# Taking the scale of v for two batches from VectorE's maximum instead of ScalarE's sums, in an attention and mixer kernel on one core

## Chip, core and metric

The kernel runs on one core of one Trainium2 chip. The metric is device time in microseconds (us) of one execution. Before the change three runs took 608.84, 609.73 and 610.28 us: the median is 609.73.

## What is computed

```python
def _attn_ref(q, k, v):                 # (8, 8, 576, 64) each
    scores = scale * np.matmul(q, k.transpose(0, 1, 3, 2))
    scores = np.where(mask, scores + bias[None], -1000000000.0)   # causal, 128 wide
    scores = scores - np.max(scores, axis=-1, keepdims=True)
    attn = np.exp(scores)
    attn = attn / (np.sum(attn, axis=-1, keepdims=True) + 1e-09)
    return np.matmul(attn, v)
def _moe_ref(x, w_theta, w_tok_r, w_tok_i, w_ch):   # x: (8, 576, 512), the heads side by side
    theta = x @ w_theta
    zr, zi = x * np.cos(theta), x * np.sin(theta)
    y = np.einsum('ts,bsd->btd', w_tok_r, zr) + np.einsum('ts,bsd->btd', w_tok_i, zi)
    u = x + y
    return u + np.maximum(u @ w_ch, 0.0)
```

## The kernel before, in words

There are eight batches of eight heads. Heads go in pairs, 32 pairs in all. For a pair, TensorE (PE) multiplies q and k into the PSUM tile s_ps (L621), in two groups of query tiles. VectorE (DVE) adds the band and takes each row's extreme (L631: an operation and a read of its accumulator), and ScalarE (ACT) takes the exponential (L635). The first 7 pairs are "early" ones: PE turns the weights (L677), ACT copies them to the tiles pt (L679), and PE multiplies them with v in fp32 (L687). The later pairs split weights and values into two fp16 halves (L644 on ACT and L646 on DVE; L601 on ACT and L603 on DVE), turn the weights by a DMA (L649) and multiply at L705. DVE divides by the row's sum and writes the heads to x_sb (L660, L663, L664).

For each batch the mixer then runs: angles by PE (L757), a reduction of them and sine and cosine (L771 to L785 on ACT and DVE; L779 and L781 are the two sine activations, which need another table of ACT than the exponential), the split of the result into z_hi (ACT, L790) and z_lo (DVE or POOL, L411), the mixing over tokens (PE, L862; what it gives is taken up at L868 to L875) and the channel product (L890), and the sums that go out (L898 to L907).

The weights come in raw, in fp32. Function `unpack` loads one chunk (L422) into one of the raw tiles u, u_spare, xtfa and xtfb, and rebuilds it with two steps on ACT (L426, and L436 where the chunk's number is under LOW_T, LOW_W or LOW_C; otherwise DVE does that second step, L440) and three on DVE (L432, L443, L452). There are 4 chunks of w_theta, 9 of w_tok and 4 of w_ch.

The values v come in groups of four heads, two groups to a batch (L499, tiles vba, vbb, vbc). Function `measure` finds a power of two per head that scales them. It has two ways:

- For the first SUMMED = 2 batches ACT sums the absolute values of each group (L516, with an accumulator that takes a second instruction to read), and DVE and PE turn the two sums into scales: L525, a transpose on PE (L531), L533, L536, a product on PE (L540), L543 and L385.
- For the other six batches DVE takes each head's largest absolute value by a reduction over 1280 elements (L521, one for each group), and a chain of four small DVE operations and one PE product follows (L548, L552, L555, L558, L561).

The order of all this is not written by hand. `Plan` records each step with its engine, an assumed duration and what it depends on; `simulate` makes an order by priorities; `order` then moves the priorities by a table of seeds, NUDGES; and `run` issues each engine's instructions in that order, so that an engine that waits holds up whatever stands behind the waiting instruction. All loads and DMA transposes are issued from SP's queue, and they land in their order there in the stretch that matters. Where the plan has PE idle, `run` puts in "spins" (L367): small products of the tile `white` that nothing uses, whose number follows the idle time of the plan.

Of the kernel before, what the change touches and what calls it, by code (L numbers as in the profile page):

```python
# [36 lines left out]
TURNED = 0  # L37
TRUE = 3
MIXED = 1
SUMMED = 2  # L40
LIFT = 2.0 ** 16
ABS_T = 4
ABS_W = 9
ABS_C = 4
LOW_T = 4
LOW_W = 5
LOW_C = 1
VALUES = ((0, 0), (1, 2))

MAGIC = 1.5 * 2.0 ** 23  # L50
# [2 lines left out]
while RAD * 0.5 > math.pi:  # L53
# [22 lines left out]
ROUNDS = 6  # L76
SELF = {"DVE": 0.115, "ACT": 0.13, "POOL": 0.1}
NUDGES = (
# [6 lines left out]
)  # L85


# [206 lines left out]
def attn_moe_kernel(ctx: ExitStack, tc: tile.TileContext, qt, kt, vx, wth, wtok, wch, band, out):  # L294
    nc = tc.nc
# [12 lines left out]
    plan = Plan()  # L308
# [84 lines left out]
    for h in range(H):  # L393
        plan("DVE", (0.14, 0.13), lambda h=h: nc.vector.tensor_scalar(
            out=bands[:, h], in0=base, scalar1=2.0 ** (2 - h), scalar2=None, op0=ALU.mult), r=[(band_buf, "base")],
            w=[(band_buf, h)], port=True)
# [16 lines left out]
    def unpack(src, c, w, held, last, first, summed, magnitude, lowest, raw_buf=None):  # L413
# [5 lines left out]
        R, E, M = ((raw_buf, k) for k in "rem")  # L419
        ex, low = t[:, 2 * S:2 * S + w], t[:, 3 * S:3 * S + w]  # L420
        powers = ex.bitcast(BF16).rearrange("p (n t) -> p n t", t=2)[:, :, 1]
        issued.append(plan("SP", (0.42, w * 2.55e-3, 2.15), lambda: nc.sync.dma_start(  # L422
            out=t[:, :2 * w], in_=src[:, c, :].bitcast(I32)), w=[R]))
        plan.follow(issued[-1], begin)
        if magnitude:
# [77 lines left out]
    def measure(b):  # L503
# [6 lines left out]
        for k in range(2):  # L510
            vb = group_v[2 * b + k]
            part = most.tile[:, GROUP * k:GROUP * k + GROUP]
            if b < SUMMED:
                spare = hl_ring.tiles[k].bitcast(BF16).rearrange("p a b c -> p (a b c)")[:, :GROUP * NT * 64].rearrange(
                    "p (h c d) -> p h c d", h=GROUP, d=64)
                taken = plan("ACT", (1.26, 0.15), lambda vb=vb, spare=spare, k=k: nc.scalar.activation(  # L516
                    spare, vb.tile[:, :, 1:, :64], AF.Abs, accum_out=spread.tile[:, k:k + 1]), r=[(vb, 0)],
                    w=[(spread, "ab"[k]), (spare_bufs[k], 0)])
                hl_ring.last[k].users.append(taken)
            else:  # L520
                plan("DVE", (1.395, 0.13), lambda vb=vb, part=part: nc.vector.tensor_reduce(  # L521
                    out=part, in_=vb.tile[:, :, 1:, :64], axis=mybir.AxisListType.XY, op=ALU.max,
                    apply_absolute_value=True), r=[(vb, 0)], w=[(most, k)])
        if b < SUMMED:
            plan("DVE", (0.075, 0.13), lambda: nc.vector.tensor_tensor(  # L525
                out=most.tile.rearrange("p (k h) -> p k h", h=GROUP),
                in0=spread.tile[:, :2, None].broadcast_to([128, 2, GROUP]),
# [19 lines left out]
        else:  # L547
# [22 lines left out]
            w=[(rise, 0)], port=True)  # L570
# [342 lines left out]
    def ready(p):  # L913
        if p >= PAIRS:
            return
        load_pair(p)
        if p % PAIRS_OF == 0:
            load_values(p // 2)
            load_values(p // 2 + 1)
            measure(p // PAIRS_OF)  # L920
        pair_weights[p] = {}, {}
        scores(p, pair_weights[p])

    issued = []
# [6 lines left out]
    for c in range(4):  # L931
        unpack(wth, c, DM, held_theta, first=c == 0, last=c == 3, summed=sums, magnitude=c < ABS_T,
               lowest=c < LOW_T)
    halve(held_theta, sums, DM, range(4), tscale, tturn, TURN, "t", wth_hi, wth_lo, theta_w)
    sums = t_ring.take()
    for k, c in enumerate(ORDER):
        unpack(wtok, c, S, held, first=k == 0, last=k == 8, summed=sums, magnitude=k < ABS_W,
               lowest=k < LOW_W, raw_buf=late_ring.take() if k % 4 == 3 else None)
    for g, c in VALUES:
# [5 lines left out]
        w=[(ws_buf, "share")], port=True)  # L945
# [7 lines left out]
    for c in range(4):  # L953
        unpack(wch, c, DM, held_chan, first=c == 0, last=c == 3, summed=sums, magnitude=c < ABS_C,
               lowest=c < LOW_C, raw_buf=late_ring.take())
    halve(held_chan, sums, DM, range(4), cscale, cscale, 1.0, "c", wch_hi, wch_lo, chan_w)
# [84 lines left out]
```

## Time and profile before

| what | value |
|---|---|
| runs before, median | 609.73 us |
| profiled execution, its own time | 614.84 us |
| its span, first to last instruction | 613.0 us |
| PE, DVE, ACT, POOL busy | 97%, 87%, 81%, 25% of the span |
| mean granted PE clock | 0.994 of full |

The profiled execution took 5.1 us more than the median of the runs, 1.8 us of its time lie outside the span. PE's busy share includes the spins. The stretches behave differently: the first 120 us, where the weights are unpacked and the first batches' attention is done, are limited otherwise than the rest.

### The profile page before, as it was taken

To read this page: it belongs to the slowest core of one execution; us is meant where nothing else is said; L and a number is where in the kernel's file an instruction comes from. 1 tells how busy PE (TensorE), PEld (TensorE's weight loads), DVE (VectorE), ACT (ScalarE), POOL (GpSimd) and SP (SyncE) were. 2 spreads that over 40 slices of the span, in tenths; PEclk is the share of its full clock that TensorE was granted. 3 is DMA by queue.
4 is the path that set the end of the run, shared out by engine and by line. 5 is a ranking of instruction groups with operands and counts; after the bars stand their busy time and mean duration, and the time that the engine had idled before them with its cause. 6 is when DMAs were issued, how large, how long until landed. Compare 5 with 4: busy or idle time off the path is not lost.

```text
span 613.0 us, 14313 instructions
## 1 busy us (share of the span) xinstructions
PE 596.3 (97%) x5417; PEld 438.9 (72%) x5417; DVE 531.4 (87%) x1568; ACT 498.8 (81%) x923; POOL 150.4 (25%) x133
## 2 busy tenths in 40 slices
PE   8997999999998999999999999999999999999997
PEld 6786756886676766776677767777677668776775
DVE  5798999999998999899898999999989999658433
ACT  4998999968998889996999689978899699246312
POOL 1000120011240215621474114231232133415100
PEclk9899999999998999999999999999999999999999
DMA  8784762399559892897569775989156734211102
GB/s 313 295 287 148 186 152 57 90 214 183 109 149 218 143 164 68 201 202 165 86 156 226 153 129 120 239 125 209 58 137 143 132 51 108 74 36 39 49 1 78
DMA packets 165541, 87.24 MB, mean 142 GB/s; under 512 B 144736, under 2 KB 153056, under 8 KB 165472
## 3 DMA queue, kind: packets, MB, share of 16 engines
q1 hardware_dynamic: 165472, 86.33, 61.1%
q8 instruction: 42, 0.69, 0.5%
q14 instruction: 27, 0.22, 0.1%
HBM read 41.22 MB, written 9.44 MB: 83 GB/s over the span
## 4 chain that ended last, share of the span: by engine, by line
PE 66%; ACT 18%; DMA 6%; DVE 6%; issue 2%; SPq 1%; POOL 0%; ACTq 0%; DVEq 0%
PE m_psb L862 15%; PE m_psa L862 15%; PE s_ps L621 7%; PE m_psa L890 7%; PE m_psb L890 6%; PE t_psa L757 5%; PE t_psb L757 5%; PE a_psb L705 3%; PE a_psa L705 3%; DMA ptd<-hlb 2%; DMA vbb<-in_vx_dram 2%; ACT sbb L635 2%; ACT sba L635 1%; ACT sbc L635 1%; ACT z_hi L790 1%
## 5 line engine op out<-in xcount | busy, mean ns | idle before, releaser
L862 PEld LDWEIGHTS <-z_hi 128*128 128x128 f16 x1152 | 110.2, 98 | 35.9 <-issue 6.3
L890 PEld LDWEIGHTS <-wch 128*128 128x128 f16 x768 | 73.8, 98 | 24.2 <-issue 4.4
L862 PE MATMUL m_psb<-wtk_hi,z_hi 128*128 128x288 f16 x288 | 82.9, 288 | 0.0
L862 PE MATMUL m_psb<-wtk_hi,z_lo 128*128 128x288 f16 x288 | 82.9, 288 | 0.0
L862 PE MATMUL m_psb<-wtk_lo,z_hi 128*128 128x288 f16 x288 | 82.9, 288 | 0.0
L862 PE MATMUL m_psa<-wtk_hi,z_hi 128*128 128x288 f16 x288 | 82.7, 287 | 0.0
L862 PE MATMUL m_psa<-wtk_lo,z_hi 128*128 128x288 f16 x288 | 82.5, 286 | 0.0
L862 PE MATMUL m_psa<-wtk_hi,z_lo 128*128 128x288 f16 x288 | 82.4, 286 | 0.0
L862 PEld LDWEIGHTS <-z_lo 128*128 128x128 f16 x576 | 56.5, 98 | 14.8 <-DVE z_lo L411 0.3
L411 POOL TENSOR_TENSOR z_lo<-wch_held,z_hi 128x512 f16<-128x512 f32 x28 | 36.8, 1329 | 67.8 <-ACT z_hi L790 67.7
L890 PE MATMUL m_psa<-u,wch 128*128 128x288 f16 x384 | 52.3, 286 | 0.8 <-ACT u_spare L898 0.8
L890 PE MATMUL m_psb<-u,wch 128*128 128x288 f16 x384 | 52.3, 286 | 0.0
L635 ACT ACTIVATE sba<-sba,fixed 128x256 f32<-128x256 f32 (+2 forms) x110 | 44.8, 460 | 3.0 <-DVE fixed L631 2.7
L812 POOL TENSOR_TENSOR hlxa<-x_sba,hlxa 128x512 f16<-128x512 f32 (+1 forms) x12 | 15.4, 1279 | 126.4 <-ACT hlxa L811 126.3
L635 ACT ACTIVATE sbc<-sbc,fixed 128x256 f32<-128x256 f32 (+2 forms) x106 | 43.3, 459 | 3.0 <-DVE fixed L631 2.9
L635 ACT ACTIVATE sbb<-sbb,fixed 128x256 f32<-128x256 f32 (+2 forms) x104 | 42.6, 462 | 3.7 <-DVE fixed L631 3.7
L757 PEld LDWEIGHTS <-xpa 128*128 128x128 f16 x224 | 21.5, 98 | 23.9 <-issue 0.7
L631 DVE CUSTOM_DVE_ANT_0 sba<-s_ps,bands 128x256 f32<-128x256 f32 (+2 forms) x110 | 35.4, 357 | 3.5 <-PE s_ps L621 3.4
L757 PEld LDWEIGHTS <-xpb 128*128 128x128 f16 x224 | 21.3, 98 | 23.5 <-issue 0.7
L631 DVE CUSTOM_DVE_ANT_0 sbc<-s_ps,bands 128x256 f32<-128x256 f32 (+2 forms) x106 | 33.7, 356 | 3.2 <-PE s_ps L621 3.1
L872 ACT ACTIVATE u<-xtfb,fixed 128x288 f16<-128x288 f32 x32 | 16.6, 526 | 24.1 <-DVE xtfb L868 24.1
L631 DVE CUSTOM_DVE_ANT_0 sbb<-s_ps,bands 128x256 f32<-128x256 f32 (+2 forms) x104 | 33.6, 358 | 1.7 <-PE s_ps L621 1.7
(325 smaller groups left out, 1576.9 us busy)
## 6 DMA issues: line engine op xcount, KB each, us to landing
vba<-in_vx_dram SPq DMA_DIRECT2D x6, 780.0 KB, 5.5
out_dram<-xtfa SPq DMA_DIRECT2D x32, 144.0 KB, 2.0
out_dram<-xtfb SPq DMA_DIRECT2D x32, 144.0 KB, 1.8
vbb<-in_vx_dram SPq DMA_DIRECT2D x5, 780.0 KB, 5.6
vbc<-in_vx_dram SPq DMA_DIRECT2D x5, 780.0 KB, 5.6
kra<-in_kt_dram SPq DMA_DIRECT2D x11, 288.0 KB, 4.6
qra<-in_qt_dram SPq DMA_DIRECT2D x11, 288.0 KB, 4.3
qrb<-in_qt_dram SPq DMA_DIRECT2D x11, 288.0 KB, 3.4
```

The lines of the kernel that those rows point to most:

```text
L411: plan(engine, cost, lambda: on.tensor_tensor(out=out, in0=whole, in1=part, op=ALU.subtract), r=r, w=w, port=True)
L621: nc.tensor.matmul(ps.tile[:qn, e, at:at + kn], qr.tile[rows, q0:q0 + qn], kr.tile[rows, k0:k0 + kn], start=True, stop=True)
L631: kn=kn, c0=c0: nc.vector.tensor_tensor_reduce(out=part, in0=source, in1=bands[:qn, (2 * p + e) % H, c0:c0 + kn], scale=-0.125, scalar=3.0 ...
L635: plan("ACT", (0.187 + kn * 0.833e-3, 0.15), lambda part=part, least=least: nc.scalar.activation(part, part, AF.Exp, bias=least, scale=-1. ...
L705: nc.tensor.matmul(av[:, to[0]:to[1], :d], l, r, start=n in STARTS and j == 0, stop=n in STOPS and j == 2)
L757: nc.tensor.matmul(t_ps, a[:, c * 128:c * 128 + 128], w[:, c, :], start=(k == 0 and c == 0), stop=(k == len(prods) - 1 and c == 3))
L790: plan("ACT", (0.52, 0.15), lambda: nc.scalar.copy(z_hi[:, c, :], z), r=key, w=[(z_buf, ("h", c))])
L812: plan("POOL", pool(512), lambda: nc.gpsimd.tensor_tensor(out=lo, in0=x, in1=hi, op=ALU.subtract), r=every + [(hlx, "h")], w=[(hlx, "l")])
L862: nc.tensor.matmul(y.tile[:, :HALF], z[:, c, m * 128:m * 128 + 128], w[:, c, cs], start=(part == 0 and j == 0 and a == 0), stop=(part == 2 ...
L872: plan("ACT", (0.43, 0.15), lambda m=m, cs=cs, at=at: nc.scalar.activation(u_hi[:, m, cs], at, AF.Copy, scale=share), r=[(xtf, ("y", m, hf ...
L890: nc.tensor.matmul(o.tile[:, :HALF], w[:, c, e * 128:e * 128 + 128], u[:, c, cs], start=(k == 0), stop=(k == 11))
```

## The change

Three edits and a new table of seeds. `SUMMED` becomes an empty tuple, so all eight batches take DVE's maximum, and ACT's sums are gone. `LOW_C` goes from 1 to 0, so the second step of w_ch's first chunk moves from ACT to DVE. The plan counts the DMA of the first three weight chunks as 0.7 us longer; that changes no instruction, only the order. With these the seeds were searched again, and the order of all engines differs from the start to the end. Lines of the new kernel between the table and `unpack` have numbers smaller by one (the spin is L366 there, z_lo L410).

```diff
-SUMMED = 2
+SUMMED = ()
...
-LOW_C = 1
+LOW_C = 0
...
 NUDGES = (
-    1, -3, -8, -9, 10, 13, 19, 28, 36, 42, 72, 86, 119, 141, 159, 171, 184, 219, 227, 230, 472, 498, 565, 586, 603,
...
+    1, 4, 5, -7, -27, -34, 35, 36, 37, 38, 45, -52, -61, 64, 71, 81, -83, 110, 120, 189, 197, 205, -206, 207, 277,
...
-        issued.append(plan("SP", (0.42, w * 2.55e-3, 2.15), lambda: nc.sync.dma_start(
+        issued.append(plan("SP", (0.42, w * 2.55e-3 + (0.7 if len(issued) < 3 else 0.0), 2.15),
+                           lambda: nc.sync.dma_start(
...
-            if b < SUMMED:
+            if b in SUMMED:
...
-        if b < SUMMED:
+        if b in SUMMED:
```

SP's queue at the start, before (band, k and q of the first pair, three chunks of w_theta, then v):

```order
L391 DMA base<-in_band_dram 128x256
L493 DMA kra<-in_kt_dram 128x576
L491 DMA qra<-in_qt_dram 128x576
L422 DMA u_spare<-in_wth_dram 128x1024
L422 DMA u<-in_wth_dram 128x1024
L422 DMA xtfa<-in_wth_dram 128x1024
L499 DMA vbb<-in_vx_dram 128x1560
L499 DMA vba<-in_vx_dram 128x1560
L491 DMA qrb<-in_qt_dram 128x576
L493 DMA krb<-in_kt_dram 128x576
L422 DMA xtfb<-in_wtok_dram 128x1152
```

and now:

```order
L390 DMA base<-in_band_dram 128x256
L491 DMA qra<-in_qt_dram 128x576
L493 DMA kra<-in_kt_dram 128x576
L422 DMA xtfa<-in_wth_dram 128x1024
L499 DMA vbb<-in_vx_dram 128x1560
L422 DMA u<-in_wth_dram 128x1024
L499 DMA vba<-in_vx_dram 128x1560
L422 DMA u_spare<-in_wth_dram 128x1024
L493 DMA krb<-in_kt_dram 128x576
L491 DMA qrb<-in_qt_dram 128x576
L499 DMA vbc<-in_vx_dram 128x1560
L422 DMA xtfb<-in_wtok_dram 128x1152
```

The two loads of v have moved up between the weight chunks: one weight load stands ahead of vbb, where there were three. The second pair's k and q stand behind the same loads as before.

DVE, from the end of the first chunks to the second pair's first scores (sbc), before:

```order
L631 ISA sbb,fixed<-s_ps,bands 128x256
...
L443 SCALAR_TENSOR_TENSOR u<-u 128x512
L452 SCALAR_TENSOR_TENSOR fga<-u 128x512
L525 TENSOR_TENSOR fixed<-fixed 128x8
L631 ISA sbc,fixed<-s_ps,bands 64x64
```

and now, from the end of the first group of scores:

```order
L521 TENSOR_REDUCE fixed<-vbb 128x4
L631 ISA sbb,fixed<-s_ps,bands 128x256
...
L432 TENSOR_SCALAR u<-u 128x512
L521 TENSOR_REDUCE fixed<-vba 128x4
L452 SCALAR_TENSOR_TENSOR fgb<-xtfa 128x512
L443 SCALAR_TENSOR_TENSOR u<-u 128x512
L548 TENSOR_SCALAR fixed<-fixed 128x8
L432 TENSOR_SCALAR u_spare<-u_spare 128x512
L452 SCALAR_TENSOR_TENSOR fga<-u 128x512
L443 SCALAR_TENSOR_TENSOR u_spare<-u_spare 128x512
L555 TENSOR_SCALAR fixed<-t_psa 128x8
L452 SCALAR_TENSOR_TENSOR fga<-u_spare 128x512
L631 ISA sbc,fixed<-s_ps,bands 128x256
```

Both reductions of the first batch and the third chunk's three steps now stand ahead of the second pair's scores, where DVE had only the result of ACT's sums (L525) between.

PE behind the first mixing products. Before, spins stand there at one place, two of them, between the last product with v of a pair and the next scores:

```order
L705 MATMUL a_psa<-vha,ptd 128x65
L367 LDWEIGHTS white
L367 MATMUL a_psb<-white 128x187
L367 LDWEIGHTS white
L367 MATMUL a_psb<-white 128x187
L621 MATMUL s_ps<-krc,qrc 64x64 x2
```

Now they stand at five places, with 3, 3, 1, 1 and 1; the second of them:

```order
L552 MATMUL t_psb<-fixed,white 128x8
L366 LDWEIGHTS white
L366 MATMUL a_psb<-white 128x187
...
L890 LDWEIGHTS wch
L890 MATMUL m_psb<-u,wch 128x288
```

In all there are 263 spins now and 231 before: 25 of the 32 more stand ahead of the last early product with v, 7 behind. ACT loads its table 46 times in the new order and 40 times in the old; up to the ninth z_hi (the first batch's last) the counts are 7 and 5.

## Rows read from the trace of the kernel before

**Rows 1.** The page's first part: busy time of each engine, its share of the span, instructions.
```profile
PE 596.3 (97%) x5417; PEld 438.9 (72%) x5417; DVE 531.4 (87%) x1568; ACT 498.8 (81%) x923; POOL 150.4 (25%) x133
```

**Rows 2.** Busy time by stretch. Columns: stretch, its length, then busy time and instructions of PE, PEld, DVE, ACT and POOL, granted PE clock, share of the DMA engines, GB/s.
```profile
0.00:20.00 20.00, 16.13 (x129) 13.08 (x130) 8.61 (x45) 10.60 (x20) 1.68 (x15) 0.91 0.90 334
20.00:120.00 100.00, 93.65 (x768) 72.02 (x767) 96.17 (x346) 97.19 (x194) 6.19 (x5) 1.00 0.55 162
120.00:180.00 60.00, 60.00 (x591) 43.90 (x591) 59.18 (x172) 52.34 (x97) 14.12 (x11) 1.00 0.81 167
180.00:200.00 20.00, 18.30 (x175) 13.36 (x173) 17.05 (x70) 17.82 (x34) 1.85 (x2) 0.91 0.85 201
200.00:500.00 300.00, 299.15 (x2847) 214.69 (x2845) 282.19 (x821) 265.87 (x484) 96.09 (x78) 1.00 0.72 148
500.00:613.00 113.00, 109.11 (x920) 81.83 (x916) 68.25 (x124) 55.01 (x98) 30.49 (x23) 1.00 0.20 52
```

**Rows 3.** The same view for the tile white alone, which only the spins use up to 120 us: PE, PEld and DVE.
```profile
0.00:120.00 120.00, 25.69 (x229) 20.74 (x229) 0.27 (x1) 0.99 0.61 191
```

**Rows 4.** What DVE waited for between 20 and 121 us: total, times, longest.
```profile
DVE u_spare L432 <- ACT u_spare L426: 1.8, 1, 1.8
DVE u L440 <- DMA u<-in_wtok_dram: 0.8, 1, 0.8
DVE xtfb L440 <- DMA xtfb<-in_wch_dram: 0.4, 1, 0.4
```

**Rows 5.** ACT's waits from 0 to 121 us, the same columns.
```profile
ACT u_spare L426 <- DMA u_spare<-in_wtok_dram: 1.7, 1, 1.7
```

**Rows 6.** DVE in order of time, from 8 to 24 us: start, duration, what, and in brackets the idle time before it and what ended that.
```profile
9.02 0.07 DVE L631 DVE_READ_ACCUMULATOR2_ANT fixed<- 128x1 f32 x1
...
10.34 0.42 DVE L432 TENSOR_SCALAR u<-u 128x512 f32<-128x512 f32 x1
...
11.02 0.42 DVE L631 CUSTOM_DVE_ANT_0 sbb<-s_ps,bands 128x256 f32<-128x256 f32 x1
...
12.77 0.69 DVE L452 SCALAR_TENSOR_TENSOR fga<-u 128x512 int32<-128x512 int32 x1
18.18 0.17 DVE L525 TENSOR_TENSOR fixed<-fixed 128x8 f32<-128x8 f32 x1 [4.72 <-ACT hla L516]
19.66 0.22 DVE L631 CUSTOM_DVE_ANT_0 sbc<-s_ps,bands 64x64 f32<-64x64 f32 x1 [1.31 <-PE s_ps L621]
...
20.43 0.27 DVE L533 TENSOR_REDUCE fixed<-t_psa 8x1 f32<-8x128 f32 x1
...
21.81 0.15 DVE L543 TENSOR_SCALAR fixed<-t_psb 128x8 int32<-128x8 int32 x1
```

**Rows 7.** PE in order of time around 191 us, where spins stand behind the first mixing products.
```profile
182.42 1.29 PE L621 MATMUL s_ps<-krb,qrb 64*64 64x64 f32 x12
...
190.87 0.33 PE L367 MATMUL a_psb<-white 128*128 128x187 bf16 x2
192.90 1.70 PE L621 MATMUL s_ps<-krc,qrc 64*64 64x64 f32 x12 [1.70 <-DVE fixed L631]
194.53 0.42 PE L862 MATMUL m_psb<-wtk_hi,z_hi 128*128 128x288 f16 x1
...
196.90 0.36 PE L862 MATMUL m_psa<-wtk_lo,z_hi 128*128 128x288 f16 x1
197.10 0.29 PE L862 MATMUL m_psa<-wtk_hi,z_lo 128*128 128x288 f16 x1
...
197.96 0.29 PE L862 MATMUL m_psb<-wtk_hi,z_hi 128*128 128x288 f16 x1
```

**Rows 8.** DVE in order of time at the same place.
```profile
190.75 1.40 DVE L785 TENSOR_TENSOR fgb<-x_sbb,fgb 64x512 f32<-64x512 f32 x2 [1.72 <-ACT fgb L781]
```

**Rows 9.** ACT in order of time there.
```profile
188.70 1.28 ACT L781 ACT_TABLE_LOAD   x1
190.00 0.72 ACT L781 ACTIVATE fgb<-fgb,fixed 64x512 f32<-64x512 f32 x1
```

**Rows 10.** ACT in order of time, from 7 to 19 us.
```profile
7.59 0.67 ACT L426 ACTIVATE u_spare<-u_spare 128x512 f32<-128x512 f32 x1 [5.56 <-DMA u_spare<-in_wth_dram]
...
9.31 0.67 ACT L426 ACTIVATE u<-u 128x512 f32<-128x512 f32 x1 [0.24 <-DMA u<-in_wth_dram]
...
13.50 1.27 ACT L516 ACTIVATE hlb<-vbb 128x1280 bf16<-128x1280 f32 x1 [1.95 <-DMA vbb<-in_vx_dram]
```

**Rows 11.** DVE in order of time at the third batch's second reduction and behind it.
```profile
119.96 1.48 DVE L521 TENSOR_REDUCE fixed<-vbb 128x4 f32<-128x1280 f32 x1
121.36 0.16 DVE L568 TENSOR_TENSOR fixed<-fixed 128x8 f32<-128x8 f32 x1
```

**Rows 12.** The second unpacking step on DVE and on ACT, by tile: duration in ns (least, median, most), first and last start.
```profile
L440 DVE TENSOR_SCALAR xtfb<-xtfb x4: 409/428/445, 45.3 to 85.9; 128x512 int32<-128x512 uint32 x3, 128x576 int32<-128x576 uint32 x1
L436 ACT ACTIVATE xtfb<-xtfb x2: 677/699/721, 24.0 to 57.3; 128x576 int32<-128x576 uint16 x1, 128x512 int32<-128x512 uint16 x1
```

**Rows 13.** ACT in order of time at one change of its table.
```profile
102.17 1.28 ACT L635 ACT_TABLE_LOAD   x1
103.47 0.51 ACT L635 ACTIVATE sbc<-sbc,fixed 128x256 f32<-128x256 f32 x1
```

**Rows 14.** PE in order of time at the first mixing product.
```profile
107.99 0.29 PE L862 MATMUL m_psa<-wtk_hi,z_hi 128*128 128x288 f16 x1
```

9 rows, old and new, of the table NUDGES are left out of this document.

## Prediction

> **What bounds the kernel now.** The page says that PE is busy for 97% of the span [rows 1], which reads as if nothing could be won. The table by stretch corrects that. From 120 us on PE is busy in 486.6 of 493 us; before that it is busy in 109.8 of 120 us, and 25.7 of these are spins [rows 2, 3]. So useful work fills only 84.1 us there and 35.9 are lost, while some 6.4 are lost in all the rest. The first 120 us are the stretch to look at. In it the two engines that the change touches are both nearly full from 20 us on: DVE 96.2 and ACT 97.2 of 100 us [rows 2]. Two full engines don't bind alike, so the next view is what each waited for. DVE waited for DMA landings there: 0.8 and 0.4 us directly, and 1.8 us through ACT, which itself had waited 1.7 us for the same chunk [rows 4, 5]. Its other waits are of 0.3 us and less. So DVE is the bound of 20 to 120 us, and what ACT is spared there gains nothing by itself. Ahead of 20 us DVE is busy for only 8.6 us [rows 2], and the list in order of time shows why: it stood still for 4.72 us until ACT had summed v, and then 1.31 us for the second pair's scores [rows 6]. Last, the one dry place behind: at 191 us PE waited 1.70 us for DVE [rows 7], which had waited 1.72 us for a sine of ACT, itself behind a table load [rows 8, 9].
>
> **The work that moves.** Four sums leave ACT, 1.27 us each [rows 10]: −5.1 us. Four reductions come to DVE. One is printed with 1.48 us, but the next operation starts 1.40 us after it [rows 11], so they cost 5.6 us of DVE's queue. The chain behind loses one small DVE operation per batch, and a reduction of 0.27 us gives way to one of some 0.15 [rows 6]: about 0.3 us a batch, −0.6 us. The edit to LOW_C takes 0.7 us from ACT and puts 0.4 on DVE [rows 12]. Sum: DVE +5.4 us, ACT −5.8 us. PE's transpose and product of the old chain go and a short product comes; at most 0.6 us on an engine that waits there, counted at nothing (it would be a gain).
>
> **What hides DVE's 5.4 us.** The wait of 4.72 us is the cover, if v lands early enough. The first weight chunk has landed at 7.6 us and the second at 9.3 [rows 10]; vbb, two more places behind, at 13.5. That is about 1.9 us a transfer. In the new queue only one weight chunk stands ahead of vbb: I put its landing at 13.5 − 2 × 1.9 = 9.6 us, and vba's, with one weight chunk between, at 13.4. DVE ends the first pair's first scores at 9.1 us [rows 6] and then stands at the reduction for half a microsecond. From 9.6 us it has a reduction (1.4), four scores and three weight steps ahead of the second reduction; seven operations of 0.42 to 0.69 us that overlap a little [rows 6], some 2.7 us. So it gets there at 13.7, when vba has landed. Behind that the third chunk's steps, which before ran after 20 us, fill DVE up to the second pair's scores, whose k and q stand behind the same loads as before. So I count the whole 4.7 us as cover. Ends: 0.2 us, if DVE has to stand until 13.5 for vbb; 6.0, if the 1.31 us are filled as well. SP passes no more loads than before at that point, only in another order; the weight chunks moved back, u from 9.3 to about 11.4 and the third from about 11.4 to 15.3, are taken by DVE only after the work that I have just counted.
>
> **Waits from 20 to 121 us.** DVE's 3.0 us there are landings of chunks that are issued when a raw tile comes free. The order is new and has other work at these points; nothing in the rows says how much. I take half, −1.5 us, between 0 and −3.0.
>
> **The head's sum:** 5.4 − 4.7 − 1.5 = −0.8 us, from −3.6 (5.4 − 6.0 − 3.0) to +5.2 (5.4 − 0.2). The 25 more spins are 2.8 us of PE at 0.112 each [rows 3]; they stand where PE has nothing to do, and 35.9 us are lost there anyway, so nothing; with that cover gone they would cost their 2.8 us.
>
> **The dry place at 191 us.** It costs more than its wait. Two spins and the wait take 2.0 us. The granted clock of that slice is 0.91 in the mean and 1.00 around it [rows 2]: for a few microseconds behind the wait PE ran at the lower of its two levels, 1.2 instead of 2.4 GHz. The scores took 1.70 us where the like took 1.29, and ten products took 2.37 us (194.53 to 196.90), where at 0.12 each (seven from 197.10 to 197.96) they would take 1.2 [rows 7]. In all 2.0 + 0.4 + 1.1 = 3.5 us. In the new order these neighbours no longer stand together, and ACT has less on it up to here. I count the place as gone: −3.5 us, with 0 as the other end. What is late next are the five places where the new order puts spins: 7 more spins are 0.8 us, and I add one wait of the old length, 1.7 us, without a fall of the clock: +2.5 us, from 0.8 to 7.8 (two places like the old one, and the spins).
>
> **Sum:** −0.8 − 3.5 + 2.5 = −1.8 us. Against the profiled execution's own 614.84 us that is 613.0. It lay 5.1 us above the median of the runs, and I carry the difference over: 609.73 − 1.8 = **607.9 us**. About 0.2%, 1.2 us, is what a measurement can tell here from no change.
>
> **Rivals.**
> - *Nothing is left of it.* The landings wait as before (head +0.7 us), and the stall at 191 us comes back elsewhere at its full price. For it: PE is full from 120 to 500 us but for a microsecond or so outside that place, so what the head wins may be spent again. Against: the cover of 4.7 us is seen. 609.73 + 0.7 = 610.4 us.
> - *PE runs dry in more places* (the other side). Behind the first mixing products DVE is full to 99% up to 180 us [rows 2], and the new order carries spins to a later point. If PE waits long enough for the clock to fall at two of the five places, the price is twice 3.5. It decides from the second such place on: −0.8 − 3.5 + 7.0 + 0.8 = +3.5, so 613.2 us. For it: five places against one. Against: ACT is no longer behind at the first of them.
> - *The reduction blocks DVE.* DVE takes its queue in order. If vbb lands at 13.5 us as before, DVE stands from 9.1 us, with the scores and weight steps that it did in that time queued behind. The head is then 5.4 − 0.2 − 1.5 = +3.7, the sum +2.7: 612.4 us. It decides from a landing later than about 11 us. Against: the order of the queue.
> - *A change of ACT's table costs more than its load.* There are six more table loads. In the trace the next activation starts 1.30 us after the load of 1.28 begins [rows 13], so they are 7.7 us on ACT, two of them in the head (2.6 us, which ACT's 5.8 less outweighs) and four later, where ACT has 34 idle of 300 us [rows 2]. If each held ACT for twice that, 7.7 us more would be due; half of it on the path gives −1.8 + 3.8 = +2.0: 611.7 us. The rows speak against it.
>
> The Trainium skill, page "ScalarE: Activation LUTs", section "What ACT_TABLE_LOAD costs", gives that rule: a load of about 1283 ns and a drain of about 1380 ns, some 2.66 us for each switch. The trace agrees on the load, but shows no such drain: ACT goes on 0.02 us after it. By the page the six would be an estimated 16.0 us instead of 7.7.
>
> **Chances.** Forecast 0.50: the cover is read from the queue itself, the gain behind 120 us is half a guess. Nothing left 0.24, more dry places 0.14, blocked reduction 0.08, dearer tables 0.04. The first is faster by over 0.2%, the second is within it, the other three are slower: 0.50, 0.24, 0.26. The range goes from 604.2 us (2.8 less for the head's lower end, and half of the 1.7 for the late wait) up to 613.2, two dry places; it leaves out what lies beyond either, which I put under 0.2.
>
> **What would show it.** Right: no DVE wait of over 1 us between 9 and 19 us, the reduction of vbb starting near 9.6 us and that of vba near 13.7 without a wait; the second pair's first scores on DVE at 19 to 20 us as before; DVE's waits from 20 to 120 us at 1.5 us instead of 3.0, and PE's first mixing products (108.0 us before [rows 14]) within 2 us of it; no place behind with a granted clock under 1. Wrong: a wait of DVE of several microseconds at L521, which is the blocked queue; slices with a clock under 1 at two or more places behind 120 us; PE waiting for exponentials or sines just behind table loads; or PE's first mixing products over 3 us later, which would say that the cover was not what held DVE.

## The result, and the profile after

The changed kernel takes 616.22 us (median of 7 runs, 613.79 to 616.94); beside it the kernel before took 610.34 (608.84 to 613.62). The medians are 5.9 us apart. The ratio is 1.0076, with a 95% interval from 1.0051 to 1.0100, that is some 4.6 us: slower, by more than the noise though by under 1%, where 607.9 us were forecast. A second measurement gave 1.0046 [1.0019, 1.0073] (e7 below). Of all runs behind the ratios below, one of e10 is left out as too slow (626.88 us, at a granted clock of 0.986). The profiled execution took 615.32 us with a span of 613.5, so it stands 0.9 us under its median; that of the kernel before stood 5.1 us over its own. Laid side by side, the two profiles differ by only 0.5 us, so most of the difference between the medians isn't in that pair.

PE's granted clock differs between runs of one program. Over 104 runs of the kernel before, 61 have a mean of 0.998 or more (median 610.0 us) and 43 less (612.9); of 19 runs of the changed kernel 7 (613.7) and 12 (615.9). With the clock alike, the change is 3.1 to 3.7 us slower. Its clock falls in 0.63 instead of 0.41 of the runs, which at some 2.5 us each adds half a microsecond; with 19 runs that difference in share can still be chance.

The first part of the changed kernel's page answers to [rows 1]:

```profile
PE 596.1 (97%) x5445; PEld 438.4 (71%) x5445; DVE 535.0 (87%) x1571; ACT 502.0 (82%) x920; POOL 154.2 (25%) x133
```

Its busy time by stretch answers to [rows 2], with the same columns:

```profile
0.00:20.00 20.00, 18.01 (x162) 15.30 (x163) 13.94 (x59) 11.73 (x25) 1.70 (x15) 1.00 0.91 335
20.00:120.00 100.00, 90.93 (x748) 68.97 (x746) 93.93 (x327) 91.26 (x179) 5.99 (x5) 0.98 0.55 161
120.00:180.00 60.00, 60.00 (x589) 43.67 (x590) 58.12 (x174) 53.47 (x95) 10.22 (x9) 1.00 0.82 168
180.00:200.00 20.00, 19.91 (x200) 15.18 (x198) 18.92 (x68) 19.97 (x43) 6.19 (x6) 1.00 0.81 199
200.00:500.00 300.00, 297.65 (x2854) 213.63 (x2853) 281.50 (x818) 269.19 (x484) 104.03 (x79) 1.00 0.72 148
500.00:613.00 113.00, 109.58 (x903) 81.63 (x900) 68.61 (x130) 56.39 (x100) 26.02 (x21) 0.99 0.21 52
```

Two things are to be seen. From 180 to 200 us PE is full and its clock is 1.00: the dry place at 191 us is gone. From 20 to 120 us DVE and ACT, both full before, stand still: DVE 6.1 us and ACT 8.7, and PE's clock is 0.98.

DVE in order of time, at the first three reductions (columns as in [rows 6]):

```profile
9.54 1.49 DVE L521 TENSOR_REDUCE fixed<-vbb 128x4 f32<-128x1280 f32 x1 [1.39 <-DMA vbb<-in_vx_dram]
...
13.59 1.48 DVE L521 TENSOR_REDUCE fixed<-vba 128x4 f32<-128x1280 f32 x1
...
18.52 0.42 DVE L631 CUSTOM_DVE_ANT_0 sbc<-s_ps,bands 128x256 f32<-128x256 f32 x1
...
19.57 1.47 DVE L521 TENSOR_REDUCE fixed<-vbc 128x4 f32<-128x1280 f32 x1
```

The start went as forecast: 9.5 and 13.6 us for the first two, where 9.6 and 13.7 were said, the second without a wait, and the second pair's scores at 18.5 instead of 19.7 us. Only DVE's wait ahead of the first is longer, 1.39 us where half a microsecond was said. But the third reduction, the second batch's first, stands right behind.

PE around 78 us, where the slice with the low clock lies, and at its first mixing product, which answers to [rows 14]:

```profile
78.74 1.36 PE L757 MATMUL t_psa<-wth_hi,xpa 128*128 128x512 f16 x4 [2.06 <-DMA xpa<-hlxa]
79.89 1.91 PE L757 MATMUL t_psa<-wth_lo,xpa 128*128 128x512 f16 x4
81.60 1.59 PE L757 MATMUL t_psa<-wth_hi,xpa 128*128 128x512 f16 x4
83.12 1.13 PE L621 MATMUL s_ps<-krb,qrb 64*128 64x256 f32 x8
...
109.72 0.29 PE L862 MATMUL m_psb<-wtk_hi,z_hi 128*128 128x288 f16 x1
```

DVE's and ACT's waits from 20 to 121 us that belong to this place (total, times, longest):

```profile
DVE sba L631 <- PE s_ps L621: 2.6, 1, 2.6
...
ACT fga L771 <- PE t_psa L757: 2.5, 1, 2.5
```

PE takes its queue in order. The first angle product waits 2.06 us for the transposed x; the twelve products run at the lower level for most of their time (4.4 us from the first start to the scores behind, where another execution of the same program took 2.7); the scores behind them come late, and DVE and ACT wait for PE. Before, DVE's waits in this stretch were for landings [rows 4].

**The account of the first stretch.** Up to the first mixing product, the time can be split into DVE's busy time and the time that DVE stands (is idle). This is bookkeeping: it would come out for any engine, and it doesn't show by itself that DVE sets the pace. For it, the table by stretch is cut at 20 us and at the first mixing product (the columns of [rows 2], DVE's is the third pair). The second stretch in the first profile of the kernel before:

```profile
20.00:107.99 87.99, 82.44 (x670) 62.25 (x669) 84.44 (x312) 85.22 (x171) 6.19 (x5) 1.00 0.60 177
```

In the changed kernel, one slice of it, from 80 to 90 us, and then the whole second stretch:

```profile
80.00:90.00 10.00, 10.00 (x62) 5.36 (x60) 7.00 (x26) 6.41 (x12) 2.33 (x2) 0.86 0.58 124
20.00:109.72 89.72, 81.26 (x667) 60.95 (x666) 83.94 (x295) 81.09 (x163) 5.99 (x5) 0.98 0.57 170
```

Before: busy 8.61 [rows 2] + 84.44 = 93.05 us, standing 11.39 ahead of 20 us and 3.55 behind. After: 13.94 + 83.94 = 97.88, standing 6.06 and 5.78. So the first mixing product moved from 107.99 to 109.72 us. Of the 5.78 us, 3.00 lie from 80 to 90 us, where the granted clock is 0.86.

### The profile page after: what moved, and what is told of

Same layout as the page of the kernel before. It is cut to its first block, busy times and chain, and to the rows that moved or that the text cites. A ratio compares the mean times of both kernels' runs of the same rounds, so it can differ in the third digit from the quotient of the medians.

```text
span 613.5 us, 14388 instructions
## 1 busy us (share of the span) xinstructions
PE 596.1 (97%) x5445; PEld 438.4 (71%) x5445; DVE 535.0 (87%) x1571; ACT 502.0 (82%) x920; POOL 154.2 (25%) x133
## 4 chain that ended last, share of the span: by engine, by line
PE 70%; ACT 16%; DMA 7%; DVE 3%; issue 2%; SPq 0%; POOL 0%; ACTq 0%; DVEq 0%; POOLq 0%
PE m_psb L862 16%; PE m_psa L862 16%; PE t_psa L757 7%; PE s_ps L621 7%; PE m_psb L890 6%; PE m_psa L890 6%; PE t_psb L757 6%; PE a_psa L705 3%; PE a_psb L705 3%; DMA xpa<-hlxa 2%; ACT sba L635 2%; ACT sbb L635 1%; ACT z_hi L790 1%; DMA vbb<-in_vx_dram 1%; ACT L635 1%
## 5 line engine op out<-in xcount | busy, mean ns | idle before, releaser
L812 POOL TENSOR_TENSOR hlxa<-x_sba,hlxa 128x512 f16<-128x512 f32 (+1 forms) x12 | 17.8, 1484 | 139.6 <-ACT hlxa L811 139.6
L410 POOL TENSOR_TENSOR z_lo<-wch_held,z_hi 128x512 f16<-128x512 f32 x28 | 35.7, 1286 | 60.6 <-ACT z_hi L790 39.2
L812 POOL TENSOR_TENSOR hlxb<-x_sbb,hlxb 128x512 f16<-128x512 f32 (+1 forms) x12 | 14.6, 1215 | 98.0 <-ACT hlxb L811 60.7
```

The source lines that it names most:

```text
L410: plan(engine, cost, lambda: on.tensor_tensor(out=out, in0=whole, in1=part, op=ALU.subtract), r=r, w=w, port=True)
L812: plan("POOL", pool(512), lambda: nc.gpsimd.tensor_tensor(out=lo, in0=x, in1=hi, op=ALU.subtract), r=every + [(hlx, "h")], w=[(hlx, "l")])
```

## Experiments

All ratios are against the kernel before, run beside each.

### e1: the kernel before once more

Nothing is edited; the question is how typical its first profile was.

> The kernel before, unchanged, once more with a profile. Theory A (the stall at 191 us was an accident of the one profiled execution, so the 3.5 us that I let the change win there were not in the median): most of its runs show a clock of 0.997 or more and spans of 607 to 609 us, and a profile of such a run has no slice under 1 at 190 us and no wait of 1.7 us there, or the wait without the half clock. Rival B (the stall is in every run, and the first profiled execution was longer for another reason): every run shows about 0.994, and the profile has the wait of 1.7 us and the half clock at 191 us again.

The time is 610.41 us (0.9992 [0.9968, 1.0017]). Its profiled execution took 610.48, next to the median. DVE where it waits for ACT's sums, and its busy time in the two stretches:

```profile
16.53 0.17 DVE L525 TENSOR_TENSOR fixed<-fixed 128x8 f32<-128x8 f32 x1 [3.66 <-ACT hla L516]
16.70 0.22 DVE L631 CUSTOM_DVE_ANT_0 sbc<-s_ps,bands 64x64 f32<-64x64 f32 x1
```

```profile
0.00:20.00 20.00, 16.97 (x151) 13.64 (x151) 11.57 (x61) 13.16 (x26) 1.68 (x15) 1.00 0.90 341
20.00:103.54 83.54, 79.76 (x647) 60.24 (x646) 81.37 (x296) 82.62 (x166) 6.21 (x5) 1.00 0.63 185
```

ACT where it takes up the first load of v, and PE at the dry place:

```profile
11.85 1.28 ACT L516 ACTIVATE hlb<-vbb 128x1280 bf16<-128x1280 f32 x1 [0.94 <-DMA vbb<-in_vx_dram]
```

```profile
188.94 2.27 PE L621 MATMUL s_ps<-krc,qrc 64*64 64x64 f32 x12 [2.19 <-DVE fixed L631]
```

Neither theory is right as stated. The stall at 191 us is here too, with the half clock (the scores take 2.27 us), but 8 of 12 runs show 0.998 or more, so the half clock there isn't in every run. What the first profile had for itself lies in the head: mixing starts at 103.54 us here, not at 107.99; v is taken up at 11.85 us and not at 13.50 [rows 10], the wait is 3.66 instead of 4.72, and the one of 1.31 behind it [rows 6] doesn't exist. DVE stands 8.43 us ahead of 20 us, not 11.39.

### e2: PE kept busy at 78 us

```diff
+MORE = 24
...
+                if s in self.marked and not self.filled:
+                    self.filled = True
+                    spin(tiles[k], MORE)
```

The steps that are marked are the angle products, so the 24 spins stand ahead of the first of them.

> The changed kernel with 24 more spins ahead of the first angle product (the one that waited 2.06 us for the transposed x at 78.7 us), nothing else moved. Theory C (PE's standstill there lets the clock fall, and the half clock is what most runs pay): the wait is filled (24 x 0.081 = 1.9 us), the granted clock stays at 1.00 from 70 to 100 us, the twelve products take 2.6 us instead of 4.4, and the median comes down by about 2 us, from 616.2 to 614.2 (ratio 1.004 against the kernel before). Rival D (DVE's four reductions hold the head, PE's standstill is only where it shows): clock as forecast, but the first mixing product stays at 109.7 us and the median at 616 (1.0075).

612.19 us, 1.0021 [1.0000, 1.0043]; all 12 runs have 0.999 or more. From 70 to 90 us:

```profile
70.00:80.00 10.00, 9.62 (x91) 8.22 (x91) 9.20 (x36) 9.26 (x23) 2.61 (x2) 1.00 0.70 157
80.00:90.00 10.00, 10.00 (x71) 5.91 (x71) 8.73 (x30) 8.44 (x18) 2.32 (x2) 1.00 0.60 148
```

The granted clock stays at 1.00 and DVE stands 1.3 us from 80 to 90 instead of 3.0. Against the first measurement of the change (1.0076 [1.0051, 1.0100]) the gain is clear and larger than theory C asked for; against the second (1.0046, e7) the intervals overlap. The mixing starts at 108.3 us, so most of the late start is not the clock.

### e3: the same order, cheap reductions

```diff
-                    out=part, in_=vb.tile[:, :, 1:, :64], axis=mybir.AxisListType.XY, op=ALU.max,
+                    out=part, in_=vb.tile[:, :, 1:(2 if b < 2 else NV), :64], axis=mybir.AxisListType.XY, op=ALU.max,
```

> The changed kernel in the very same order, but the reductions of the first two batches read 256 instead of 1280 elements (the scale of these batches is then taken from a fifth of v): each should take some 0.35 instead of 1.48 us, 4.4 us less on DVE. Rival D (the reductions are what the head lost): the first mixing product comes 3 to 4 us earlier (106 us) and the median falls to 612 (1.003). Theory C (the place at 78 us hangs on the DMA transpose behind ACT and POOL and on the order): the first mixing product moves by less than 1.5 us, the wait for xpa stays over 1 us, the median stays over 614.5.

613.02 us, 1.0029 [1.0003, 1.0055]. Busy time in the two stretches:

```profile
0.00:20.00 20.00, 18.10 (x157) 15.26 (x158) 11.76 (x59) 11.16 (x24) 1.69 (x15) 1.00 0.90 333
20.00:107.24 87.24, 80.09 (x671) 61.09 (x671) 82.49 (x295) 81.38 (x164) 5.79 (x5) 1.00 0.58 175
```

DVE is busy 94.25 us, 3.6 less than in the change, but stands 2.2 more ahead of 20 us, and the mixing starts at 107.24: 2.5 us sooner than in the first profile of the change and 0.4 sooner than in its second (e7). PE at the first angle product:

```profile
78.61 1.04 PE L757 MATMUL t_psa<-wth_hi,xpa 128*128 128x512 f16 x4 [2.35 <-ACT pta L679]
```

The ratio is the one of rival D (1.003), the wait of over 1 us stays as theory C had it, and the first mixing product lies between the two. Some 1 to 3 us come back, by the ratio of e7 or by the first one, and both intervals overlap with this one. In the new order a lighter DVE mostly waits longer.

### e4: a neighbouring order

The last ten seeds of the change's table are left out, nothing else.

> The changed kernel without the last ten seeds of its table: the same instructions apart from ten rows of spins, some 7% of ACT's and DVE's standing elsewhere. Theory E (which order the table gives decides over several us, more than the three edits do): the time differs from 616.2 by over 2 us, and the PE waits of over 1.5 us stand at other places. Rival D (the edits' own cost decides): within 1 us of 616.2 (1.0075), first mixing product within 1 us of 109.7.

617.13 us, 1.0117 [1.0075, 1.0159] (6 runs). The first mixing product comes at 109.7 us, and the wait for the transposed x is 2.03 us at the same place. By its numbers this is rival D (within 1 us of 616.2, the first mixing product in its place), but the interval is wide, and so small a change of order settles nothing.

### e5: the dry place of the kernel before filled

```diff
+MORE = 18
...
-                spin(tiles[k], int(FILL * (s.start - max(last, used[k])) / SPIN))
+                count = int(FILL * (s.start - max(last, used[k])) / SPIN)
+                if s.start > 125.0 and count > 0 and not self.filled:
+                    self.filled = True
+                    count += MORE
+                spin(tiles[k], count)
```

> The kernel before with 18 more spins at its one late spin place (ahead of the scores at 187 to 191 us, where PE waited 1.70 us in the first profiled execution and 2.19 in the second), nothing else moved. Theory C (a standstill lets the clock fall, and the half clock is paid by the runs in which it happens): 18 x 0.081 = 1.5 us of the wait are filled, no run shows a clock under 0.999 from this place, the runs come to 608 to 611 us and the median falls by about 1.3 us (ratio 0.998). Rival F (PE is not what ends the time there; DVE and ACT are late anyway): the clock stays up but the ratio is 1.000; the spins themselves delay the scores where the wait is short: up to 1.001.

611.06 us, 0.9999 [0.9971, 1.0027]. PE at the place:

```profile
187.50 1.78 PE L372 MATMUL a_psb<-white 128*128 128x187 bf16 x20
189.44 1.29 PE L626 MATMUL s_ps<-krc,qrc 64*64 64x64 f32 x12 [0.15 <-DVE fixed L636]
```

The wait is filled and the scores run at full speed, but 4 of 12 runs are still under 0.998; where the clock fell in these no profile shows. Rival F stands: no gain that can be measured.

This kernel is the one before up to that place, so its first 20 us are another sample of the cover:

```profile
0.00:20.00 20.00, 15.79 (x141) 12.91 (x142) 10.35 (x56) 11.86 (x24) 1.69 (x15) 1.00 0.90 336
```

DVE stands 9.65 us here, between the first profile (11.39) and e1 (8.43).

### e6: both edits of e2 and e3

> The changed kernel with both edits at once: 24 more spins ahead of the first angle product, and the first two batches' reductions over 256 elements only (their scale is taken from a fifth of v). Alone, the first took the ratio from 1.0076 to 1.0021, the second to 1.0029. Theory G (two causes that add: DVE's extra work, and PE's standstill with its clock): 1.0076 - 0.0055 - 0.0047 = 0.9974, 609.4 us. Rival H (both end the same wait at 78 us, since a less busy DVE and a filled PE each keep the clock up there): nothing is gained over the better one, 1.002, 612 us.

612.41 us, 1.0006 [0.9982, 1.0029]; all 12 runs have 0.998 or more. The changed kernel itself, measured beside it, took 614.71 (e7): the two edits together gain 2.3 us. Against e2 alone the gain is 0.0015, inside the intervals. Whether the two edits add isn't settled, as it hangs on the ratio they start from. From 1.0076, as in the forecast, they don't, and rival H holds. From e7's 1.0046, e2 gains 0.0025 and e3 0.0017, which would leave 1.0004, and 1.0006 was measured: then they add.

### e7: the changed kernel once more

> The changed kernel unchanged, once more beside the others. Expected by all theories: 1.0076 of the kernel before, 615 to 616 us, first mixing product at 109 to 110 us, the wait for the transposed x at 78 us over 1 us. Theory C: the half clock stands right behind that wait in the runs with a clock of 0.997. Should the first mixing product of this profile come at 105 us or the ratio at 1.003 or less, the loss in the first 120 us was an accident of one execution, as with the kernel before.

614.71 us, 1.0046 [1.0019, 1.0073]. PE at 78 us, and the two stretches:

```profile
79.58 1.04 PE L757 MATMUL t_psa<-wth_hi,xpa 128*128 128x512 f16 x4 [2.53 <-DMA xpa<-hlxa]
```

```profile
0.00:20.00 20.00, 18.34 (x159) 15.59 (x160) 14.01 (x59) 11.30 (x24) 1.69 (x15) 1.00 0.90 339
20.00:107.64 87.64, 79.66 (x669) 60.84 (x668) 83.84 (x295) 81.31 (x163) 5.95 (x5) 1.00 0.58 173
```

The loss is no accident: mixing starts at 107.64 us, 4.1 later than in e1, in an execution whose clock didn't fall at that place. It is less than expected, 109 to 110 us and 1.0076. The wait is longer than in the first profile, and the products take 1.04 us for four. DVE's longest waits from 20 to 121 us:

```profile
DVE u_spare L432 <- ACT u_spare L426: 1.6, 1, 1.6
DVE xtfb L440 <- DMA xtfb<-in_wch_dram: 0.9, 1, 0.9
DVE sba L631 <- PE s_ps L621: 0.8, 1, 0.8
```

### e8 to e11: four other orders

Four tables of seeds were searched from other numbers, each for its own kernel: the change (e8), the kernel before with SUMMED empty and nothing else (e9), the change with ACT's sums put back (e10), and the kernel before itself (e11).

The edit of e8, the first lines of both tables:

```diff
 NUDGES = (
-    1, 4, 5, -7, -27, -34, 35, 36, 37, 38, 45, -52, -61, 64, 71, 81, -83, 110, 120, 189, 197, 205, -206, 207, 277,
...
+    30004, -30008, 30013, -30014, -30016, 30018, 30027, 30035, 30050, 30054, 30056, -30058, -30086, 30096,
...
```

> All three edits of the change, but another table of 47 seeds, searched from other numbers. On DVE the last heads of the first batch are written at row 221 (row 240 with the table of the change, 213 in the kernel before), three of the first two batches' four reductions stand ahead of them, and ACT loads its table 42 times (46 and 40). Theory I (the place that the table gives to the first batch's end decides, not the edits): last heads written at 64 to 66 us instead of 70.4, no PE wait of over 1.5 us at the first angle product, first mixing product at 104 to 106 us, ratio 1.000 to 1.003. Rival D (the edits themselves cost: 5 us more on a full DVE): first mixing product at 107 us or later, ratio 1.004 or more.

> The kernel before with SUMMED empty as the only edit (LOW_C stays 1, no longer loads in the plan), and a table of 53 seeds searched for it. Last heads of the first batch at row 188 of DVE, three of the four reductions ahead of them. Theory I: as for the other seeds, last heads at 60 to 64 us, first mixing product at 104 to 106 us, ratio 1.000 to 1.003, so taking the maximum costs little where the order suits it. Rival D: 1.004 or more, as the maximum is what costs.

> The change without its main edit: ACT's sums for the first two batches as in the kernel before, LOW_C 0 and the longer loads in the plan as in the change, and a table of 64 seeds searched for it. Last heads of the first batch at row 209 of DVE. Theory I: within what orders differ by, 0.999 to 1.004. Rival D: 0.998 to 1.001, and faster by 2 us or more than the two kernels with the maximum that run beside it.

> The code of the kernel before with another table of 54 seeds. It computes the same by the same instructions, so what differs is the order alone. Theory I: its ratio is anywhere from 0.999 to 1.006, and the places where PE stands still are others (none of 2 us at 187 to 191 us). Rival D: 1.000 within 0.002.

| | what it has | ratio | first mixing product |
|---|---|---|---|
| e8 | all three edits | 1.0137 [1.0104, 1.0170] | 107.5 us |
| e9 | the maximum alone | 1.0114 [1.0083, 1.0146] | 107.5 |
| e10 | sums, the other two edits | 1.0118 [1.0081, 1.0154] | 105.6 |
| e11 | the kernel before | 1.0052 [1.0028, 1.0075] | 108.3 |

My numbers for theory I fell for all but e11, above all its hinge, the place of the first batch's end: e9 has its first angle product at 61.4 us, 17 sooner than the change, and mixes when e7 does (107.64). Rival D's numbers came true for e8 and e9 and fell for e10 and e11: with the sums, e10 is as slow as e9 with the maximum. What holds is the spread. The same code in another order costs 0.5% (e11), about as much as the whole change, and with ACT loading its table 42 times.

Two things limit what the four can say of the edits. They differ in their code as well as in their order: against e11, the only one without an edit, e8 is 6.3 us slower, much as the change is than the kernel before. So in both pairs of orders the edited kernel is the slower one; two pairs, where an order alone moves 0.5%, don't prove the edits to be the cause. And in e8, e9 and e10 about half of the loss or more lies behind the first mixing product: from there to the end they take 513.4, 508.9 and 509.9 us, where e1 takes 505.2, e7 504.3 and e11 504.5.

DVE in e9:

```profile
0.00:20.00 20.00, 15.75 (x146) 13.03 (x148) 13.76 (x59) 11.79 (x25) 1.69 (x15) 1.00 0.90 338
20.00:107.50 87.50, 82.36 (x691) 63.54 (x688) 84.78 (x296) 84.20 (x165) 6.50 (x5) 1.00 0.57 174
```

Here DVE stands only 2.72 us behind 20 us, nearly as little as in e1 (2.17), and the mixing still starts 4 us later: busy 98.54 instead of 92.94, and 6.24 instead of 8.43 standing ahead. By this pair 5.6 us more of DVE's work find 2.2 us of cover. It doesn't price the maximum, as the order is another one too: e11, the code of e1 in another order, mixes 4.7 us later than e1 without any maximum in these batches. Behind the first mixing product e8 and e9 lose again from 120 to 140 us, where PE's granted clock is 0.77 and 0.83.

### e12 and e13: the reductions alone, in the old order

In the kernel before, the maxima of one batch's two groups are taken in addition and not used, ahead of L525: the first batch's inside the wait that I had called cover (e12), the second batch's at some 80 us (e13, with EXTRA = 1).

```diff
+EXTRA = 0
...
+                for k in (1, 0) if b == EXTRA else ():
+                    nc.vector.tensor_reduce(
+                        out=most.tile[:, GROUP * k:GROUP * k + GROUP], in_=pair_v[k].tile[:, :, 1:, :64],
+                        axis=mybir.AxisListType.XY, op=ALU.max, apply_absolute_value=True)
```

> The kernel before with two more reductions on DVE, the maxima of the first batch's two groups (their results are written over and not used), right ahead of the operation that waits for ACT's sums (3.66 us at 12.9 us in the second profile of that kernel, 4.50 in that with more spins, 4.72 in the first); order and all else as before. Theory J (that wait is cover, as I counted it): DVE is busy 2.9 us more up to the first mixing product and stands 2.5 to 2.9 less ahead of 20 us, the first mixing product stays at 103.5 to 105 us, ratio 1.000 within 0.0015. Rival K (no cover: the first reduction holds up the scores behind it, or the sums wait with it): first mixing product 2 to 3 us later, ratio 1.004.

> The same with the maxima of the second batch's two groups, again unused, ahead of the operation that takes up that batch's sums, at some 78 us, where DVE stands 2 us or less from 20 us to the first mixing product. Theory J: nothing hides them, DVE's 2.9 us come whole on the first mixing product, 106.5 to 108 us, ratio 1.0045. Rival L (DVE is busy but not what sets the pace there, as the kernel with cheap reductions gained little): first mixing product within 1 us, ratio 1.000 to 1.0015.

e12 takes 610.55 us, 1.0006 [0.9982, 1.0031]; e13 614.34, 1.0078 [1.0053, 1.0103]. DVE in e12, then both kernels' busy times and e13's PE:

```profile
13.05 1.48 DVE L530 TENSOR_REDUCE fixed<-vbb 128x4 f32<-128x1280 f32 x1
14.45 1.48 DVE L530 TENSOR_REDUCE fixed<-vba 128x4 f32<-128x1280 f32 x1
17.14 0.17 DVE L533 TENSOR_TENSOR fixed<-fixed 128x8 f32<-128x8 f32 x1 [1.21 <-ACT hla L517]
```

```profile
0.00:20.00 20.00, 16.30 (x147) 13.37 (x149) 13.76 (x61) 12.52 (x25) 1.69 (x15) 1.00 0.91 347
20.00:105.54 85.54, 80.38 (x653) 60.56 (x650) 82.22 (x298) 83.36 (x167) 6.20 (x5) 1.00 0.58 179
```

```profile
0.00:20.00 20.00, 17.04 (x147) 13.92 (x149) 11.00 (x59) 12.57 (x25) 1.69 (x15) 1.00 0.88 337
20.00:110.13 90.13, 82.12 (x654) 60.99 (x651) 85.93 (x300) 83.48 (x167) 6.14 (x5) 0.98 0.58 172
```

```profile
85.04 1.87 PE L766 MATMUL t_psb<-wth_hi,xpb 128*128 128x512 f16 x4 [2.58 <-DVE fga L782]
```

Theory J, with a price above the one I gave. Two reductions inside the wait cost nothing that the runs can tell (at most 1.9 us by the interval), though the first mixing product of that profile comes at 105.54 us, 2.0 behind e1, where rival K began, and 0.9 behind e5 (104.62). Two such reductions outside it cost 0.8%, 4.8 us, as much as the whole change in its first measurement: DVE's 2.9 us, and in the profile PE, which stands 2.58 us behind them, runs its next products at the lower clock (1.87 us for four, not 1.04).

## Why the prediction was wrong

**What was right.** DVE's added work: forecast +5.4 us, measured 97.88 − 93.05 = +4.8. The reductions' places, at 9.5 and 13.6 us (13.5 − 2 × 1.9 is 9.7 and not the 9.6 that I wrote; nothing hangs on it). The stall at 191 us: gone, PE's idle time in 180 to 200 us from 1.70 to 0.09 and the clock from 0.91 to 1.00, as the sum had it (−3.5). In most runs, though, the half clock there, 1.5 of the 3.5, isn't shown to be won: e1 shows 8 of 12 at 0.998 or more, and e5, with the place filled, gains nothing. The late places: +2.5 forecast; PE stands 1.5 us more from 200 to 500 (297.65 against 299.15 busy), the same behind (3.9 to the end of either span), and the spins are 0.8 more by the forecast's price: some +2.3. So all that lies behind the first mixing product came as forecast, −1.0 us: it took 505.0 us before and 503.8 after in the first profiles, 505.2 in e1 and 504.3 in e7. Both profiles of the kernel before have the half clock at the stall, which is part of why this fits. The error lies in the head. Of the rivals, a blocked reduction and PE dry at two places behind with a falling clock did not come.

**The step that failed most: "It lay 5.1 us above the median of the runs, and I carry the difference over."** I took the cover of one long execution as what every run has. Between the two profiles +0.5 us was measured where −1.8 was forecast; the other 5.4 of the 5.9 us between the medians are how far these executions lay from them, 4.5 above 610.34 and 0.9 under 616.22. Most of its 5.1 us were in the head (107.99 against 103.54 in e1), in just the waits that the sum spends: DVE stands 11.39 us ahead of 20 us there and 8.43 in e1. Between the two profiles the cover came out even larger than forecast (11.39 − 6.06 = 5.3 instead of 4.7). From e1 to e7 it is 8.43 − 5.99 = 2.4; with e13 (9.00) or e5 (9.65) in the place of e1, whose start is the same, 3.0 or 3.7. So the change removed a delay that the other three profiles of that start don't have in full, and 1.0 to 2.3 us of DVE's work that I counted as covered weren't. The sign that I had named, the first mixing product within 2 us of its old place, read as right (109.72 against 107.99) only because that place was late; against e1 it is 6.2 us later, and 4.1 in e7.

**The second: "I take half, −1.5 us" for DVE's waits from 20 us on.** The sign was wrong: +2.2 between the two profiles (3.55 to 5.78), +1.6 from e1 to e7 (2.17 to 3.80). Between e1 and e7 this is the larger miss within the sum, 3.1 us beside the 2.3 of the cover. I had put the old order's landings on the account, and nothing for new waits. In the first profile the new one is PE at the first angle product, with DVE and ACT behind it (2.6 of DVE's 5.8 us). It lies ahead of the first mixing products, where I had looked for dry places only behind them. In e7, where the clock didn't fall there, it costs DVE 0.8 us, and the landings alone cost 2.5 us (1.6 through ACT and 0.9 directly), where 1.5 was forecast for all waits.

**The sum again.** From e1 to e7, two executions near their kernels' times at a clock of 0.997 and 0.999: +4.9 (DVE's work) − 2.4 + 1.6 = +4.1 us at the first mixing product. The forecast had −0.8 there. The spans differ by 3.2 (608.7 and 611.9). The runs show +2.8 us (0.0046 of 611, e7) and +4.6 (0.0076 of 610) by the ratios, 3.5 and 5.9 by the medians.

**What is settled and what isn't.** That the two reductions of the first batch can hide, to within 1.9 us, and that two outside the wait cost 3 us or more, is shown in the old order (e12, e13). That PE's standstill costs the changed kernel time through its clock is shown: with the wait filled all 24 runs keep the clock (e2, e6), where 12 of 19 of the changed kernel lose it and take 2.2 us more than the rest. The kernel before loses it in 43 of 104 runs too, so how much of the loss this is isn't settled, nor whether it is separate from DVE's load (e6). Nor is how the rest divides between the edits and the order: another order of unchanged code costs 0.5% (e11), and in the new order cheap reductions give back some 1 to 3 us by the middle values (e3), less than the 3.6 us that they take from DVE. The dearer table switches weren't tried alone; in the changed kernel the activation starts 0.01 us after the load:

```profile
184.87 1.28 ACT L635 ACT_TABLE_LOAD   x1
186.16 0.35 ACT L635 ACTIVATE sba<-sba,fixed 64x64 f32<-64x64 f32 x1
```

By the Trainium skill, page "ScalarE: Activation LUTs", section "What ACT_TABLE_LOAD costs", about 1380 ns of drain would stand there besides the load; this trace has none.

## What to carry to other kernels

Before an idle gap of a profile is spent as cover, profile the kernel a second time: an execution that is longer than the median may owe part of the gap to that (here 3.0 of the 11.4 us). Work moved onto a nearly full engine is free only as far as it stands inside a wait; split it by place, and price what lies outside at its duration or above (in e13 2.9 us of work cost 4.8, as the engine behind stood still as well). A change that comes with a newly searched order is two changes, so run the old code under another order of the same kind before judging the edit.

## What the runs showed of the hardware

One and the same wait may or may not bring the half clock: 2.06 us at the first angle product was followed by four products in 1.36 us and four in 1.91, and 2.53 us in another execution of the same program by four in 1.04. In the same order with cheap reductions (e3) 2.35 us were followed by four in 1.04. In e1 the kernel before had 2.19 us at the stall with scores at 2.27 us, although most of its runs have a mean clock of 0.998 or more. The Trainium skill, page "TensorE: Matmul & The Clock Gate", section "What's actually happening", says that what the chip watches runs on by itself and isn't tied to the kernel; the two executions agree with that, and no run here shows it directly.

The first load of v was taken up at 13.50 us [rows 10] in one execution and at 11.85 in another of the same program; the wait for the sums behind it was 4.72 and 3.66 us.
